# A new order of operations for the start, the repeated step and the end of a tiled recurrence with a max-out layer

## Chip, cores and metric

One core of one Trainium2 chip. The metric is the device time of one execution in microseconds (us), of the slowest core, here the only one. Medians and ranges of several executions are given. A profiled execution also has a *span*, from the first to the last counted instruction; it is 1.7 to 1.8 us shorter than the time of the same execution.

## The reference

```python
def _attn_ref(q, k, v, f_logit):                 # each (4, 8, 768, 48), float32
    f = 1.0 / (1.0 + np.exp(-f_logit))
    for t in range(S):
        state = f[:, :, t, :, None] * state + einsum('bhd,bhe->bhde', k[:, :, t], v[:, :, t])
        y[:, :, t] = einsum('bhd,bhde->bhe', q[:, :, t], state)

def _moe_ref(x, w1, w2, w_out):                  # x (3072, 384), w1, w2 (384, 1024), w_out (1024, 384)
    return np.maximum(x @ w1, x @ w2) @ w_out
```

The kernel cuts the sequence into 24 tiles of 128 positions (six for each of four batches; batches alternate). It uses max(a, b) = b + relu(a - b): with wd = w1 - w2 and w2o = w2 · w_out, the output is x · w2o + relu(x · wd) · w_out. So wd and w2o are built once, at the start, while tiles 0 and 1 are already under way.

## The kernel before

All operations have short names, and the order of every engine's queue is the order in which the names stand in three strings. The PROLOGUE sets up and runs the first tiles, the STEP is repeated with a growing tile number, the EPILOGUE ends. The traces show an engine's operations taken in that order: in run e2, further down, VectorE stood idle for 2.86 us ahead of a product whose load had not landed, and what stands behind it came after.

```python
PROLOGUE = """
setup 0  setup 2  setup 1  lf 0  lwo 2  lw2 4  lw2 3  lw2 2  lw2 0  lw2 5  e 0  lv 0  lw1 2
... (cut)
wdp 1  x 0  trqe 1  xT 0  lf 3  woc 3  a 1  am 1  lv 2  wdp 4  ln 2  w2o 10  w2o 9  w2oe 1
lq 3  cum 2  xTe 0  w2o 8  wdp 3  w2o 11  lk 3  wd 0  w2oe 2  lf 4  wd 5  d0 0  w2oe 0  ei 2
... (cut)
"""
STEP = """
lq 1  lv 1  lf 4  out -9  lk 2  st -4  d0 -1  cum 1  g0 -1  a 0  d1 -1  ei 1  am 0  fl 1
e 2  ed 1  o0 -1  g1 -1  kpv 1  qp 1  qp 0  y 0  ln 2  tmp -3  o1 -1  x 0  xT 0  tr 1  xTe 0
sa -2  tre 1  ob -1  v 1  qpv -2
"""
# what the names do (cut)
def sub_wd(n, eng=nc.vector):                    # "wd" on VectorE, "wdp" on GpSimd
    eng.tensor_sub(wd[:, j, cs], w1_f[:, j, cs], w2_f[:, j, cs])       # line 170, 128 x 512
def v_v(i):                                      # "v": VectorE, cast of v to bf16
    nc.vector.tensor_copy(vb, ld[i]["v"]...)                           # line 204
def m_kp(i, eng):                                # "kp" on GpSimd, "kpv" on VectorE
    eng.tensor_mul(s["kp"][:, :, 0:D], ld[i]["k"], s["ei"]...)         # line 232, 128 x 384
def m_qp(i, eng):                                # "qp" on GpSimd, "qpv" on VectorE
    eng.tensor_mul(s["qp"][:, :, 0:D], ld[i]["q"], s["ed"]...)         # line 237
# "lf lk lq lv n": loads of tile n (192 KB each); "lw1 lw2 lwo n": pieces of the weights;
# "tr": TensorE's transposes of kp and qp; "a": scores; "am": their mask (VectorE); "y": am·v + state;
# "x": y to bf16 (ScalarE); "d0 d1": x·wd in two halves; "g0 g1": relu (ScalarE);
# "o0 o1": the output (TensorE); "ei ed fl": exponentials (ScalarE); "tmp st": state (VectorE, GpSimd)
```

## Time and profile before

| | kernel before |
|---|---|
| time, median of 3 | 147.08 us (146.97 to 147.21) |
| span of the profiled execution | 145.5 us |
| TensorE busy | 127.8 us, 88% |
| first d / second d (tile 0 / tile 1) | 26.28 / 30.24 us |
| one tile in the middle | 4.96 us |

Two marks are used from here on. *d of tile n* is the first product with wd: TensorE can't start the first before wd is there. *o of tile n* is the first matmul of the output; it comes once a tile, so the differences between two kernels at each o show where time is won or lost. The lines of this profile stand in the prediction below.

### The profile page before, as it was taken

To read this page: it belongs to the slowest core of one execution; us is meant where nothing else is said; L and a number is where in the kernel's file an instruction comes from. 1 tells how busy PE (TensorE), PEld (TensorE's weight loads), DVE (VectorE), ACT (ScalarE), POOL (GpSimd) and SP (SyncE) were. 2 spreads that over 40 slices of the span, in tenths; PEclk is the share of its full clock that TensorE was granted. 3 is DMA by queue.
4 is the path that set the end of the run, shared out by engine and by line. 5 is a ranking of instruction groups with operands and counts; after the bars stand their busy time and mean duration, and the time that the engine had idled before them with its cause. 6 is when DMAs were issued, how large, how long until landed. Compare 5 with 4: busy or idle time off the path is not lost.

```text
span 145.5 us, 4481 instructions
## 1 busy us (share of the span) xinstructions
PE 127.8 (88%) x1817; PEld 100.9 (69%) x1817; DVE 104.4 (72%) x189; ACT 86.9 (60%) x202; POOL 56.2 (39%) x85
## 2 busy tenths in 40 slices
PE   0009697799999999999999999999999999999980
PEld 0005663687788878877888788888878877887680
DVE  7802868768697789677977887797779777979530
ACT  3336647765857697458656855775587558653430
POOL 8202278002836152454255325523552454245000
PEclk9999999999999999999999999999999999999999
DMA  4999999999998998999999999989999898914141
GB/s 112 310 326 206 289 299 293 177 202 190 157 205 149 207 189 153 199 148 221 199 234 185 229 229 194 216 174 227 183 205 223 188 232 163 268 44 162 59 162 56
DMA packets 106277, 28.61 MB, mean 197 GB/s; under 512 B 100496, under 2 KB 104720, under 8 KB 106256
## 3 DMA queue, kind: packets, MB, share of 16 engines
q1 hardware_dynamic: 106256, 28.32, 95.4%
q8 instruction: 14, 0.23, 0.7%
q14 instruction: 7, 0.06, 0.1%
HBM read 23.59 MB, written 4.72 MB: 195 GB/s over the span
## 4 chain that ended last, share of the span: by engine, by line
PE 86%; DMA 4%; ACT 2%; DVE 2%; SPq 2%; issue 1%
PE o L347 28%; PE d L329 24%; PE tr L244 7%; PE a L262 5%; DMA w_f<-in_moe_w_dram 4%; PE y L307 3%; PE xtp L317 3%; PE cum L209 3%; PE y L302 2%; PE sa L276 2%; PE w2op L187 2%; PE warm L386 2%; PE w2tp L177 1%; SPq L150 1%; DVE wd L170 1%; PE cum L211 1%
## 5 line engine op out<-in xcount | busy, mean ns | idle before, releaser
L237 POOL TENSOR_TENSOR qp<-qt,ed 128x384 bf16<-128x384 f32 x22 | 24.6, 1120 | 73.2 <-ACT ed L221 45.7
L336 ACT ACTIVATE gT<-d 128x512 bf16<-128x512 f32 x48 | 29.1, 606 | 34.1 <-PE d L329 34.0
L329 PE MATMUL d<-xT,wd 128*128 128x128 bf16 x576 | 39.7, 219 | 1.7 <-DVE wd L170 1.2
L347 PE MATMUL o<-wo,gT 128*128 128x384 bf16 x184 | 37.4, 325 | 0.0
L329 PEld LDWEIGHTS <-wd 128*128 128x128 bf16 x576 | 33.0, 98 | 4.4 <-DVE wd L170 1.6
L267 DVE TENSOR_TENSOR am<-a,mask 128x1024 bf16<-128x1024 f32 x24 | 29.4, 1224 | 1.2 <-PE a L262 1.2
L321 DVE COPY xT<-xtp 128x384 bf16<-128x384 bf16 x24 | 8.6, 357 | 20.1 <-PE xtp L317 20.1
L347 PEld LDWEIGHTS <-gT 128*128 128x128 bf16 x184 | 16.2, 97 | 9.0
L291 POOL TENSOR_TENSOR st<-tmp,fl 64x192 bf16<-64x192 f32 x40 | 20.5, 512 | 2.5 <-DVE tmp L284 1.0
L253 DVE COPY trs<-tr 128x1024 bf16<-128x1024 bf16 (+1 forms) x27 | 16.9, 631 | 3.1 <-PE tr L244 1.2
L209 PE MATMUL cum<-ell,ut 128*128 128x384 bf16 x24 | 8.0, 333 | 10.6 <-ACT ell L200 10.6
L196 ACT ACTIVATE e<-ft 128x384 f32<-128x384 f32 x24 | 12.7, 529 | 4.2 <-DMA ft<-in_f_logit_dram 4.1
L347 PE MATMUL o<-w2o,xT 128*128 128x384 bf16 x69 | 15.0, 326 | 0.0
L312 ACT CAST x<-y 128x384 bf16<-128x384 f32 x24 | 11.5, 480 | 5.0 <-PE y L307 4.9
L232 DVE TENSOR_TENSOR kp<-kt,ei 128x384 bf16<-128x384 f32 x21 | 13.1, 626 | 0.4 <-ACT ei L217 0.3
L221 ACT ACTIVATE ed<-cum 128x384 f32<-128x384 f32 x24 | 12.0, 498 | 2.1 <-PE cum L211 2.1
L200 ACT ACTIVATE ell<-e 128x384 bf16<-128x384 f32 x24 | 13.0, 540 | 0.2
L352 DVE COPY ob<-o 128x384 f32<-128x384 f32 x23 | 12.6, 548 | 0.5 <-PE o L347 0.5
L211 PEld LDWEIGHTS <-ell 128*128 128x128 bf16 x80 | 5.0, 98 | 10.6 <-issue 9.3
L217 ACT ACTIVATE ei<-cum 128x384 f32<-128x384 f32 x24 | 11.7, 487 | 0.0
L307 PE MATMUL y<-vb,am 128*128 128x48 bf16 x192 | 11.3, 184 | 0.0
L284 DVE TENSOR_TENSOR tmp<-sa,st 128x384 f32<-128x384 f32 x20 | 11.0, 551 | 0.0
(56 smaller groups left out, 176.7 us busy)
## 6 DMA issues: line engine op xcount, KB each, us to landing
ft<-in_f_logit_dram SPq DMA_DIRECT2D x24, 192.0 KB, 4.1
vt<-in_v_dram SPq DMA_DIRECT2D x24, 192.0 KB, 4.7
qt<-in_q_dram SPq DMA_DIRECT2D x24, 192.0 KB, 4.8
kt<-in_k_dram SPq DMA_DIRECT2D x24, 192.0 KB, 4.3
out_dram<-ob SPq DMA_DIRECT2D x23, 192.0 KB, 3.3
w_f<-in_moe_w_dram SPq DMA_DIRECT2D x12, 256.0 KB, 5.5
wo_f<-in_moe_w_out_dram SPq DMA_DIRECT2D x4, 384.0 KB, 4.8
out_dram<-obl SPq DMA_DIRECT2D x2, 96.0 KB, 1.6
```

The costliest lines, as they stand in the source:

```text
L196: nc.scalar.activation(e, ld[i]["f"].rearrange("p h d -> p (h d)"), AF.Exp, scale=-1.0)
L200: nc.scalar.activation(ell[:, :, 0:D], st[i]["e"].rearrange("p (h d) -> p h d", h=H), AF.Ln, bias=1.0)
L232: eng.tensor_mul(s["kp"][:, :, 0:D], ld[i]["k"], s["ei"].rearrange("p (h d) -> p h d", h=H))
L237: eng.tensor_mul(s["qp"][:, :, 0:D], ld[i]["q"], s["ed"].rearrange("p (h d) -> p h d", h=H))
L253: nc.vector.tensor_copy(s["tr"][:, n:n + len(sel)], psum.pop(("tr" + sel, i)))
L267: nc.vector.tensor_mul(am.rearrange("p o n c -> p (o n) c"), psum.pop(("a", i)).rearrange("p o n c -> p (o n) c"), mask)
L291: nc.gpsimd.tensor_mul(st_b[b][(c + 1) % 2][r, :, e], st[i]["tmp"][r, :, e], st[i]["fl"][r, :].unsqueeze(2).to_broadcast([DP, NP, D]))
L307: nc.tensor.matmul(out=y[:, ds], lhsT=am[:, o, p, :], rhs=vb[:, ds], start=(c == 0), stop=(c == 0 or o == 1))
L329: nc.tensor.matmul(out=ps[:, n, :], lhsT=wd[:, j, f * C:(f + 1) * C], rhs=st[i]["xT"][:, j, :], start=(j == 0), stop=(j == JG - 1))
L336: nc.scalar.activation(s["g"][:, half * 4:half * 4 + 4, :], psum.pop(("d", half, i)), AF.Relu)
L347: nc.tensor.matmul(out=psum["o", i], lhsT=l() if callable(l) else l, rhs=r, start=(n == 0), stop=(n == len(mms) - 1))
L352: nc.vector.tensor_copy(t, psum.pop(("o", i)))
```

## The change

Its intent: in the first seven steps, VectorE's instructions with two operands in SBUF are to be kept clear of GpSimd's. Beside one they take longer in the trace of the kernel before: a kp 0.72 and 1.07 us instead of 0.55, a subtraction 1.65 instead of 0.68; and four st of GpSimd beside such a kp take 2.54 us instead of 4 x 0.54. *Blocked* means this observation and no more, and so does *lock*. Weight pieces and tile loads are issued in a new order, all subtractions for wd but one go to VectorE, and in the step kp goes to GpSimd and qp to VectorE. The stores of tiles 15 to 22 move from the EPILOGUE into the step. Only the three strings change. The diff, cut:

```diff
 PROLOGUE = """
-setup 0  setup 2  setup 1  lf 0  lwo 2  lw2 4  lw2 3  lw2 2  lw2 0  lw2 5  e 0  lv 0  lw1 2
+setup 0  setup 2  setup 1  lwo 2  lw2 2  lw2 1  lw2 3  lw1 4  lw2 4  lf 0  woc 2  lw2 5
 ... (cut)
-lq 3  cum 2  xTe 0  w2o 8  wdp 3  w2o 11  lk 3  wd 0  w2oe 2  lf 4  wd 5  d0 0  w2oe 0  ei 2
+tr 1  lv 2  woc 3  w2o 7  tre 1  w2o 11  lq 3  e 2  w2o 9  w2o 10  ln 2  a 1  lk 3  wd 1
+w2oe 2  cum 2  w2oe 1  lf 4  wd 5  d0 0  w2oe 0  am 1  d1 0  g0 0  lv 3  ed 2  fl 2  v 1
+ei 2  o0 0  g1 0  lq 4  kp 2  y 1  o1 0  x 1  lk 4  qpv 2  xT 1  trk 2  xTe 1  trq 2  trke 2
 ... (cut)
+o1 5  x 6  lq 9  xT 6  tr 7  xTe 6  cum 8  tre 7  lf 10  fl 8  ei 8  ob 5  v 7  lv 11  lq 10
 STEP = """
-lq 1  lv 1  lf 4  out -9  lk 2  st -4  d0 -1  cum 1  g0 -1  a 0  d1 -1  ei 1  am 0  fl 1
-e 2  ed 1  o0 -1  g1 -1  kpv 1  qp 1  qp 0  y 0  ln 2  tmp -3  o1 -1  x 0  xT 0  tr 1  xTe 0
-sa -2  tre 1  ob -1  v 1  qpv -2
+d0 -1  cum 1  g0 -1  a 0  d1 -1  ed 1  am 0  qpv -3  ei 1  fl 1  g1 -1  kp 1  qp -3  o0 -1
+tmp -3  y 0  qpv 1  o1 -1  x 0  st -3  e 2  xT 0  tr 1  ln 2  xTe 0  sa -2  tre 1  ob -1
+v 1  lk 5  lf 5  lq 4  out -9  lv 4
 EPILOGUE = """
-out 19  out 20  out 16  out 18  st 22  st 23  st 21  out 21  out 22  out 15  sa 23  out 17
-lo 1  lo 3  lob1 0  lo 0  lo 2  lout 1  lob0 0  fl 23  lout 0
+st 23  st 22  st 21  tmp 23  lo 1  lo 3  sa 23  lob1 0  lo 0  sa 22  lo 2  lout 1  lob0 0
+lout 0
```

More of the change, by code (lines that the diff above doesn't have):

```diff
@@ L17 @@
 PROLOGUE = """
-setup 0  setup 2  setup 1  lf 0  lwo 2  lw2 4  lw2 3  lw2 2  lw2 0  lw2 5  e 0  lv 0  lw1 2
-woc 2  lw2 1  lq 0  lk 0  lf 1  lwo 0  lk 1  w2ca 5  ln 0  w2ca 2  cum 0  lwo 1  w2ca 0
-warm 6  lq 1  fl 0  ei 0  w2ca 3  lw1 1  w2c 1  w2ca 4  ed 0  lf 2  qp 0  w2T 6  w2T 2  lwo 3
-w2Te 6  w2T 0  kp 0  w2Te 2  w2T 4  w2Te 0  w2T 3  lw1 4  e 1  w2T 5  w2Te 3  trk 0  w2Te 4
-trq 0  ln 1  w2T 1  w2T 7  w2Te 1  lw1 3  cum 1  trke 0  fl 1  ei 1  trqe 0  ed 1  a 0  lw1 0
-kpv 1  woc 0  w2Te 5  v 0  w2Te 7  w2o 1  lw1 5  woc 1  am 0  w2o 0  w2o 2  sa 0  lv 1  qp 1
@@ L24 @@
-w2o 5  tmp 0  w2o 3  w2o 6  lq 2  wdp 2  w2o 4  w2o 7  trk 1  lk 2  e 2  y 0  trke 1  trq 1
-wdp 1  x 0  trqe 1  xT 0  lf 3  woc 3  a 1  am 1  lv 2  wdp 4  ln 2  w2o 10  w2o 9  w2oe 1
-lq 3  cum 2  xTe 0  w2o 8  wdp 3  w2o 11  lk 3  wd 0  w2oe 2  lf 4  wd 5  d0 0  w2oe 0  ei 2
-d1 0  g0 0  lv 3  v 1  ed 2  y 1  fl 2  x 1  lq 4  qpv 2  o0 0  g1 0  xT 1  o1 0  lk 4  kpv 2
-trq 2  xTe 1  trk 2  ob 0  d0 1  lf 5  e 3  trke 2  trqe 2  d1 1  ln 3  g0 1  lq 5  v 2
-a 2  cum 3  g1 1  am 2  fl 3  ed 3  lv 4  o0 1  ei 3  qp 3  y 2  lk 5  kpv 3  o1 1  x 2
@@ L30 @@
-xT 2  tr 3  lf 6  e 4  xTe 2  sa 1  d0 2  tre 3  ln 4  ob 1  lq 6  cum 4  a 3  v 3  ed 4
-d1 2  g0 2  am 3  lv 5  qp 4  ei 4  g1 2  o0 2  tmp 1  lv 6  kp 4  fl 4  y 3  o1 2  x 3
-st 0  lk 6  e 5  xT 3  tr 4  xTe 3  ln 5  sa 2  d0 3  tre 4  lf 7  ob 2  cum 5  g0 3  a 4
-d1 3  lf 8  v 4  ei 5  am 4  ed 5  g1 3  qp 5  lv 7  o0 3  tmp 2  y 4  kpv 5  st 2  o1 3
-x 4  lq 7  fl 5  e 6  xT 4  tr 5  st 1  ln 6  xTe 4  lk 7  sa 3  d0 4  tre 5  ob 3  cum 6
-lf 9  a 5  v 5  fl 6  ei 6  d1 4  am 5  g0 4  lq 8  ed 6  g1 4  o0 4  tmp 3  y 5  lk 8  kp 6
@@ L36 @@
-qpv 6  o1 4  x 5  lf 11  e 7  xT 5  tr 6  xTe 5  ln 7  sa 4  d0 5  tre 6  lv 8  ob 4  cum 7
-a 6  v 6  ed 7  d1 5  lk 9  g0 5  am 6  e 8  g1 5  lf 10  qp 7  o0 5  tmp 4  ei 7  y 6  fl 7
-lq 9  kpv 7  o1 5  x 6  ln 8  xT 6  tr 7  xTe 6  lv 9  e 9  cum 8  tre 7  ln 9  ob 5  lk 11
-v 7  lk 10  lq 10  lq 12  lf 12
+setup 0  setup 2  setup 1  lwo 2  lw2 2  lw2 1  lw2 3  lw1 4  lw2 4  lf 0  woc 2  lw2 5
+lv 0  lf 1  lw2 0  lq 0  lk 0  lwo 1  w2c 4  wd 4  lwo 0  e 0  w2ca 3  lq 1  w2ca 2  ln 0
+w2ca 1  lw1 3  v 0  cum 0  ei 0  lw1 0  w2ca 5  e 1  lw1 2  w2c 0  w2T 7  ed 0  w2T 2  w2Te 7
@@ new lines @@
+ln 1  w2T 5  w2Te 2  fl 0  lk 1  qp 0  w2T 6  w2Te 5  w2T 4  w2Te 6  w2T 1  w2Te 4  cum 1
+lwo 3  kp 0  w2T 0  warm 2  w2Te 0  lf 2  woc 1  w2Te 1  tr 0  ei 1  ed 1  lw1 1  sa 0  fl 1
+w2T 3  tre 0  woc 0  tmp 0  a 0  lw1 5  qp 1  w2Te 3  w2o 2  w2o 0  lv 1  wd 3  w2o 1  w2o 3
+lk 2  wdp 0  am 0  w2o 6  lq 2  y 0  w2o 4  x 0  w2o 5  lf 3  kp 1  xT 0  w2o 8  xTe 0  wd 2
+tr 1  lv 2  woc 3  w2o 7  tre 1  w2o 11  lq 3  e 2  w2o 9  w2o 10  ln 2  a 1  lk 3  wd 1
+w2oe 2  cum 2  w2oe 1  lf 4  wd 5  d0 0  w2oe 0  am 1  d1 0  g0 0  lv 3  ed 2  fl 2  v 1
@@ new lines @@
+ei 2  o0 0  g1 0  lq 4  kp 2  y 1  o1 0  x 1  lk 4  qpv 2  xT 1  trk 2  xTe 1  trq 2  trke 2
+d0 1  trqe 2  lf 5  e 3  ob 0  a 2  ln 3  d1 1  g0 1  am 2  lv 4  cum 3  g1 1  v 2  ed 3
+lq 5  o0 1  ei 3  y 2  qp 3  fl 3  o1 1  x 2  lk 5  kpv 3  xT 2  tr 3  xTe 2  sa 1  lf 6
+e 4  d0 2  tre 3  ln 4  ob 1  a 3  g0 2  lf 7  v 3  cum 4  am 3  d1 2  ei 4  ed 4  lv 5
+g1 2  tmp 1  o0 2  qp 4  y 3  lk 6  kpv 4  o1 2  x 3  st 0  fl 4  xT 3  tr 4  lq 6  e 5
+xTe 3  sa 2  d0 3  ln 5  tre 4  lf 8  ob 2  cum 5  a 4  v 4  ed 5  d1 3  fl 5  am 4  g0 3
@@ new lines @@
+lv 6  qp 5  ei 5  g1 3  o0 3  st 1  lq 7  kpv 5  y 4  tmp 2  o1 3  x 4  lk 7  e 6  xT 4
+tr 5  ln 6  xTe 4  sa 3  d0 4  tre 5  lk 8  e 7  ob 3  cum 6  g0 4  a 5  lv 7  v 5  d1 4
+ei 6  am 5  ed 6  ln 7  lf 9  kp 6  o0 4  g1 4  tmp 3  y 5  fl 6  st 2  lq 8  qpv 6  o1 4
+x 5  xT 5  st 3  tr 6  xTe 5  lk 9  sa 4  cum 7  tre 6  d0 5  ed 7  ob 4  lv 8  a 6  v 6
+g0 5  d1 5  am 6  ei 7  lf 11  e 8  g1 5  o0 5  qpv 7  fl 7  ln 8  y 6  lv 9  tmp 4  kp 7
+o1 5  x 6  lq 9  xT 6  tr 7  xTe 6  cum 8  tre 7  lf 10  fl 8  ei 8  ob 5  v 7  lv 11  lq 10
@@ L40 @@
+lk 10  lv 10  lk 11  lq 11  lv 12  lf 12  lq 12  lk 12
 """
 STEP = """
-lq 1  lv 1  lf 4  out -9  lk 2  st -4  d0 -1  cum 1  g0 -1  a 0  d1 -1  ei 1  am 0  fl 1
-e 2  ed 1  o0 -1  g1 -1  kpv 1  qp 1  qp 0  y 0  ln 2  tmp -3  o1 -1  x 0  xT 0  tr 1  xTe 0
-sa -2  tre 1  ob -1  v 1  qpv -2
+d0 -1  cum 1  g0 -1  a 0  d1 -1  ed 1  am 0  qpv -3  ei 1  fl 1  g1 -1  kp 1  qp -3  o0 -1
+tmp -3  y 0  qpv 1  o1 -1  x 0  st -3  e 2  xT 0  tr 1  ln 2  xTe 0  sa -2  tre 1  ob -1
+v 1  lk 5  lf 5  lq 4  out -9  lv 4
```

## The prediction

> **What bounds the kernel now.** I read the page first, then the waits of TensorE, then the timeline: of one step in the middle, of the first 30 us, and of the end. The page:
>
> ```profile
> span 145.5 us, 4481 instructions
> PE 127.8 (88%) x1817; PEld 100.9 (69%) x1817; DVE 104.4 (72%) x189; ACT 86.9 (60%) x202; POOL 56.2 (39%) x85
> PE   0009697799999999999999999999999999999980
> DMA  4999999999998998999999999989999898914141
> PE 86%; DMA 4%; ACT 2%; DVE 2%; SPq 2%; issue 1%
> ```
>
> TensorE fills every slice from the ninth to the last but one. The chain that ended last is 86% TensorE. What TensorE waits for:
>
> ```profile
> PE cum L209 <- ACT ell L200: 10.6, 1, 10.6
> PE d L329 <- DVE wd L170: 1.2, 1, 1.2
> PE w2op L187 <- ACT wo L166: 0.9, 2, 0.6
> PE a L262 <- DVE trs L253: 0.7, 1, 0.7
> ```
>
> All of these waits lie in the first 27 us (columns: total, times, longest). Now the middle, by two first halves of d, one step apart:
>
> ```profile
> 84.50 0.83 PE L329 MATMUL d<-xT,wd 128*128 128x128 bf16 x12
> 89.46 0.83 PE L329 MATMUL d<-xT,wd 128*128 128x128 bf16 x12
> ```
>
> One tile takes 4.96 us. Start to start, the parts are d 0.67+0.68, cum 0.33, a 0.33, o 0.98+0.81, y 0.37, xtp 0.17, tr 0.45, sa 0.17: the sum is 4.96, so nothing is left between them. A new order of other engines' work can't shorten this; it can only break it. From the first d to the end TensorE loses little: o of tiles 1 and 2 start at 32.42 and 37.39, 4.97 apart, where a tile without the state term (0.17 less) needs 4.79, so 0.18 is lost there. The next intervals are 4.79, 4.96, 4.96. The end (from 135.78) has about 1 us of waits that belong to the chain of the last tile.
>
> So the time is (start of the first d) + about 119.2 us, and the first d is where gain can come from:
>
> ```profile
> 20.00 2.50 POOL L170 TENSOR_TENSOR wd<-w_f 128x512 bf16<-128x512 f32 x2
> 23.18 2.50 POOL L170 TENSOR_TENSOR wd<-w_f 128x512 bf16<-128x512 f32 x2 [0.69 <-DMA w_f<-in_moe_w_dram]
> 24.57 2.26 DVE L170 TENSOR_TENSOR wd<-w_f 128x512 bf16<-128x512 f32 x2
> 26.28 1.51 PE L329 MATMUL d<-xT,wd 128*128 128x128 bf16 x24 [1.23 <-DVE wd L170]
> ```
>
> The two subtractions of VectorE take 1.65 and 0.68 us (longest and shortest of that group). The long one began at 24.57, inside GpSimd's fourth, which lasts to 25.68; the first d waits for it 1.23 us.
>
> [...]
>
> ```profile
> 42.37 1.00 POOL L237 TENSOR_TENSOR qp<-qt,ed 128x384 bf16<-128x384 f32 x1 [2.42 <-issue]
> 43.06 0.72 DVE L232 TENSOR_TENSOR kp<-kt,ei 128x384 bf16<-128x384 f32 x1
> 43.32 2.54 POOL L291 TENSOR_TENSOR st<-tmp,fl 64x192 bf16<-64x192 f32 x4
> ```
>
> kp takes 0.55 us when free; here it ends 0.41 us after GpSimd's qp ends (43.78 against 43.37). It comes before the st that is queued behind qp: four st take 2.54 us instead of 4 x 0.54. At 33.43 a kp takes 1.07 in the same way.
> [...] Here: qp 1.00 us against 0.55.
> [...] Here 12 of 128 columns take 0.67 us, 56 ns each[...]; the six "warm" matmuls of 512 columns begin 0.43 us apart at 11 us[...].
>
> **The change, part by part.**
>
> *The step.* TensorE's order is the same, instruction for instruction. kp moves to GpSimd and qp to VectorE; on ScalarE ed comes ahead of ei, and e after x; tmp comes ahead of the product on VectorE. I lay the measured durations on the step that begins with d at 84.50. ScalarE: g0 85.37, ed 85.86, ei 86.24 to 86.73, g1 about 86.75. GpSimd: kp 86.86 to 87.86. VectorE: am to 87.17, tmp 87.08 to 87.63, then qp blocked until 87.86, ending 88.28 (plus 0.41, as above). TensorE transposes kp at 88.84 and qp at 89.06: 0.8 us to spare for qp, 1.0 for kp. x is ready for xtp as before; ln ends about 89.6 and cum starts at 90.1. So 4.96 us stay 4.96: gain 0.
>
> *Loads.* The first 24 transfers are the same set in another order (8 of 192 KB, 12 of 256 KB, 4 of 384 KB), so the last weight piece lands at the same time. I fit them on the traced waits that end with a landing (f at 3.5, a w2 piece at 9.5 and one at 11.9, f at 14.6, q at 19.05, f at 20.5). My estimate from these is 0.92, 0.8 and 1.2 us each, from 2.0 us, plus 1.3 us to land. It gives 23.7+1.3 = 25.0 for the 24th and 24.2 for the 23rd. In the new order these are w1 pieces 5 and 1; piece 1 gates the first half of d, piece 5 the second.
>
> *The first d.* w1 piece 4 is subtracted early, pieces 3, 2, 1, 5 on VectorE and only 0 on GpSimd, at about 19.6, so no GpSimd work meets the last two: 0.68 us each instead of 1.65 for one. Piece 1: 24.25 to 24.9. The other gates: f of tile 2 is 22nd and lands at 23.4, e and ln to 24.5; the last cast of wo (21st, landing 22.5) is 0.83 long, to 23.35; three pairs of w2op (0.33 each) to 24.4; a 0.33 and cum 0.33 to 25.1. So the first d starts at about 25.1 (26.28 before): 1.2 us earlier. If landings are 0.5 us later than my fit, at 25.6.
>
> *What is given back.* ScalarE does ed, fl, ei of tile 2 ahead of g1 of tile 0: g1 ends at about 28.0, and o of tile 0, which wants it at 27.8, waits about 0.25. q of tile 2 lands at about 27.9, its product on VectorE is blocked by GpSimd's kp (27.55 to 28.55) and ends at 28.97; the second d (30.41 before) starts at about 29.4. In tile 3 kp on VectorE still meets qp on GpSimd: 0.17 lost, like the 0.18 of before. From here the step runs with a lead of 0.8 to 1.0 us.
>
> *Four fewer "warm" matmuls.* Before, they lay in a stretch in which TensorE waited for ScalarE's casts (13.1 to 13.5). Gain 0 by themselves.
>
> *The end.* The outs come in order, one per step, instead of in the epilogue; before, three were issued at 139 to 140.3, just ahead of the last two stores. With less ahead of them the last stores may land up to 0.2 us earlier; I count 0.05.
>
> Sum: 1.2 - 0.25 - 0.1 + 0.05 = 0.9 us by the fit, about 0.4 with late landings. I take 0.8: 147.08 - 0.8 = 146.3 us.
>
> **Rivals.** (a) *The start is bound by the transfers, and nothing is gained.* For: the same bytes come ahead of the first d, the loads of tiles 2 to 4 follow about 1 us apart with little lead (f of tile 3 lands at 28.9, wanted at 29), and tile 0's own chain starts later (f of tile 0 is 7th instead of 1st; cum at 11.6 instead of 10.57). Against: before, 1.2 us were lost after the last landing. It would make 146.9 to 147.2.
> (b) [...] If st went ahead of the blocked qp, qp would end at about 89.35, TensorE would wait 0.3 us a step, over 17 steps 5 us: 152. Against: 43.06, where VectorE went first.
> [...]
> (d) *More than I see.* If the chain of tile 0 and the weights lets d start at the landing of piece 1 itself, and everything after it is at its floor, 145.4.
>
> **Range and chances.** The middle is fixed at 4.96 a tile, so only 0 to 1.5 us are at stake: 145.4 to 147.1 holds (a), the sum and (d). Over 2% faster means under 144.1, a first d at about 23.3, before its weights have landed: 0.03. Over 2% slower needs (b)[...]: 0.02. Within 2%: 0.95.
>
> **What would show it right or wrong.** Right: steps of 4.96 us between d's in the middle; all wd on VectorE near 0.68 us; the first d at 25.0 to 25.7; the second near 29.4; VectorE's qp in the middle at 0.55 to 0.75 us. Wrong: TensorE waiting for trs or tr in the middle (b); [...] a first d that waits for x, wo or w2o at 26 or later (a). I'd be wrong altogether if the step were not 4.96 us any more.

## The result, and the profile after

The changed kernel took **147.93 us** (median of 4, 147.76 to 148.17), the kernel before on the same chip 147.15 (146.97 to 147.23): ratio 1.0056, 95% interval 1.0037 to 1.0075. Ratios here are the mean time of one kernel's fast runs over that of the other's of the same rounds, so not quite the ratio of the medians. That is within 2%, as said, but 0.8 us slower where 0.8 us faster was predicted, and above the range.

Its page and its waits of TensorE (total, times, longest):

```profile
span 146.0 us, 4482 instructions
PE 128.0 (88%) x1813; PEld 100.9 (69%) x1813; DVE 108.7 (74%) x190; ACT 88.9 (61%) x201; POOL 56.4 (39%) x83
PE 81%; ACT 5%; DMA 5%; DVE 3%; issue 2%; SPq 2%; POOL 1%
PE cum L209 <- ACT ell L200: 12.3, 1, 12.3
PE y L307 <- DVE am L267: 0.6, 2, 0.3
PE tr L244 <- POOL kp L232: 0.5, 1, 0.5
```

TensorE's work is the same. Its first wait, for tile 0's chain, has grown from 10.6 to 12.3 us; it ends before 12.5 us, ahead of the first d. The long wait for wd (1.2 us before) is gone, as intended. New ones have come: for kp on GpSimd, and for am on VectorE, a wait that the kernel before doesn't have. In the chain that ended last, TensorE's share fell from 86% to 81%. Now the timeline of the start (columns: start, duration, engine, line, operation, out<-in, tile and type, count; in brackets the idle time before it and what ended it), as it answers to the wd and d lines of before:

```profile
24.57 1.49 DVE L170 TENSOR_TENSOR wd<-w_f 128x512 bf16<-128x512 f32 x2
25.50 1.50 PE L329 MATMUL d<-xT,wd 128*128 128x128 bf16 x24
28.77 0.99 POOL L232 TENSOR_TENSOR kp<-kt,ei 128x384 bf16<-128x384 f32 x1 [5.95 <-ACT x L312]
29.45 0.73 DVE L237 TENSOR_TENSOR qp<-qt,ed 128x384 bf16<-128x384 f32 x1 [1.99 <-DMA qt<-in_q_dram]
...
30.23 0.23 PEld L244 LDWEIGHTS <-qp 128*128 128x128 bf16 x4 [0.19 <-DVE qp L237]
30.50 0.83 PE L329 MATMUL d<-xT,wd 128*128 128x128 bf16 x12
```

The two last subtractions are no longer blocked (1.49 us for both, 2.26 before) and the first d starts at 25.50, 0.78 earlier. But tile 2's products wait for their loads: VectorE stood idle 1.99 us until q of tile 2 had landed (29.3; k at 28.6). The second d, which stands behind the transposes of tile 2, starts at 30.50. The same stretch of the kernel before:

```profile
28.18 0.56 DVE L237 TENSOR_TENSOR qp<-qt,ed 128x384 bf16<-128x384 f32 x1 [1.07 <-ACT ed L221]
28.65 0.55 DVE L232 TENSOR_TENSOR kp<-kt,ei 128x384 bf16<-128x384 f32 x1
30.24 1.50 PE L329 MATMUL d<-xT,wd 128*128 128x128 bf16 x24
```

There, in this profile, the product of q waits for ScalarE's ed, not for a load. So of 0.78 us nothing is left at the second d, and 0.26 us are lost on top. The middle is as predicted: a step of 4.96 us.

```profile
80.50 0.83 PE L329 MATMUL d<-xT,wd 128*128 128x128 bf16 x12
85.46 0.72 PE L329 MATMUL d<-xT,wd 128*128 128x128 bf16 x10
```

A fifth of a microsecond more is lost in tile 3 (o of tile 1 to o of tile 2 takes 5.14 us, 4.94 before). Most of the rest comes where the prologue meets the step (the *seam*, around 56 us): o of tile 6 to o of tile 7 takes 5.45 us instead of 4.96. The timeline there, after:

```profile
55.76 0.48 ACT L217 ACTIVATE ei<-cum 128x384 f32<-128x384 f32 x1
56.32 1.00 POOL L232 TENSOR_TENSOR kp<-kt,ei 128x384 bf16<-128x384 f32 x1 [2.71 <-ACT ei L217]
56.46 1.08 DVE L204 CAST vb<-vt 128x384 bf16<-128x384 f32 x1
...
58.73 0.22 PE L307 MATMUL y<-vb,am 128*128 128x48 bf16 x2 [0.32 <-DVE am L267]
```

and before:

```profile
55.99 0.35 DVE L204 CAST vb<-vt 128x384 bf16<-128x384 f32 x1
```

ei of tile 8 now comes ahead of ScalarE's other work ("fl 8 ei 8" at the end of the PROLOGUE), so GpSimd's kp of tile 8 starts 0.14 us ahead of VectorE's cast of v of tile 7. The cast, which has *one* operand, takes 1.08 us instead of 0.35 and ends 0.22 us after kp (57.54 against 57.32); am is late (57.46; before it began at 56.25), and y waits.

### The profile page after: what moved, and what is told of

Same layout as the page of the kernel before. It is cut to its first block, busy times and chain, and to the rows that moved or that the text cites. A ratio compares the mean times of both kernels' runs of the same rounds, so it can differ in the third digit from the quotient of the medians.

```text
span 146.0 us, 4482 instructions
## 1 busy us (share of the span) xinstructions
PE 128.0 (88%) x1813; PEld 100.9 (69%) x1813; DVE 108.7 (74%) x190; ACT 88.9 (61%) x201; POOL 56.4 (39%) x83
## 4 chain that ended last, share of the span: by engine, by line
PE 81%; ACT 5%; DMA 5%; DVE 3%; issue 2%; SPq 2%; POOL 1%
PE o L347 25%; PE d L329 23%; PE tr L244 8%; PE a L262 5%; DMA ft<-in_f_logit_dram 5%; PE y L307 3%; PE cum L209 3%; PE xtp L317 3%; PE sa L276 2%; PE y L302 2%; PE w2tp L177 2%; DVE am L267 2%; PE w2op L187 2%; SPq L150 1%; ACT gT L336 1%
## 5 line engine op out<-in xcount | busy, mean ns | idle before, releaser
L232 POOL TENSOR_TENSOR kp<-kt,ei 128x384 bf16<-128x384 f32 x21 | 21.0, 1000 | 54.4 <-ACT fl L227 30.6
L267 DVE TENSOR_TENSOR am<-a,mask 128x1024 bf16<-128x1024 f32 x24 | 29.3, 1222 | 0.1
L291 POOL TENSOR_TENSOR st<-tmp,fl 64x192 bf16<-64x192 f32 x40 | 25.9, 647 | 1.6
L209 PE MATMUL cum<-ell,ut 128*128 128x384 bf16 x24 | 8.2, 341 | 12.3 <-ACT ell L200 12.3
L237 DVE TENSOR_TENSOR qp<-qt,ed 128x384 bf16<-128x384 f32 x19 | 14.3, 755 | 2.0 <-DMA qt<-in_q_dram 2.0
L211 PEld LDWEIGHTS <-ell 128*128 128x128 bf16 x80 | 5.1, 99 | 12.3 <-issue 11.2
L237 POOL TENSOR_TENSOR qp<-qt,ed 128x384 bf16<-128x384 f32 x5 | 5.0, 998 | 21.3 <-ACT ed L221 19.2
```

Source lines behind the costliest of these rows:

```text
L232: eng.tensor_mul(s["kp"][:, :, 0:D], ld[i]["k"], s["ei"].rearrange("p (h d) -> p h d", h=H))
L237: eng.tensor_mul(s["qp"][:, :, 0:D], ld[i]["q"], s["ed"].rearrange("p (h d) -> p h d", h=H))
L267: nc.vector.tensor_mul(am.rearrange("p o n c -> p (o n) c"), psum.pop(("a", i)).rearrange("p o n c -> p (o n) c"), mask)
L291: nc.gpsimd.tensor_mul(st_b[b][(c + 1) % 2][r, :, e], st[i]["tmp"][r, :, e], st[i]["fl"][r, :].unsqueeze(2).to_broadcast([DP, NP, D]))
```

## The experiments

Fifteen runs were made, in four groups, each group on one chip and beside runs of the kernel before. Theories: **S** (supply): the loads of tile 2 come too late, and take back what the first d gained. **V** (seam): v's cast is blocked beside GpSimd's kp (1.08 us instead of 0.35), and this costs 0.49 us. **O** (order): the new order of work on the engines itself gives back what the first d gained. **E** (end): the stores issued ahead of the last ones cost time before.

### First group: loads, seam, end

**e1, the changed kernel with its first 24 transfers in the old order.**

```diff
 # changed kernel: same operations, the 24 first loads take the old sequence of kinds
-... lwo 2  lw2 2  lw2 1  lw2 3  lw1 4  lw2 4  lf 0  lw2 5  lv 0  lf 1  lw2 0  lq 0  lk 0 ...
+... lf 0  lwo 2  lw2 2  lw2 1  lw2 3  lw2 4  lw2 5  lv 0  lw1 4  lw2 0  lq 0  lk 0  lf 1 ...
```

> The new kernel, with its first 24 transfers put in the order of kinds of the old kernel (tile, wo, five w2, ...); nothing else changed. Theory L (the supply): in the new kernel k, q of tile 2 and f of tile 3 landed at 28.6, 29.3, 30.2 us, 1.0 us later than in the old one (28.2 for the later of k and q, 29.1), and this cost 0.87 us between the first and the second d. If the order of the first 24 transfers makes this, they land again at 28.2 and 29.1, the second d starts at 29.6 to 29.9 instead of 30.50, and the kernel takes 147.1 to 147.4 instead of 147.9. Theory O (the order of ScalarE's and GpSimd's work loses it, whatever lands when): the second d stays at 30.3 to 30.6 and the time at 147.7 to 148.1.

Measured: 149.08 us (fast runs, 148.92 to 150.03; one of the six was slow), ratio 1.0154 (1.0100 to 1.0209). A miss. GpSimd's subtraction waits 2.44 us for its piece and holds back kp of tile 1; the first d comes at 27.27.

**e2, the kernel before with its first 24 transfers in the new order.** (The same edit the other way round.)

> The old kernel, with its first 24 transfers in the order of kinds of the new kernel. Theory L: k and q of tile 2 land 0.5 to 1.0 us later and the time is 147.5 to 148.1. Theory O: the time stays within 0.2 us of 147.15.

Measured: 153.55 us, ratio 1.0419 (1.0370 to 1.0468). A miss. VectorE, whose queue is taken in order, stands still 2.86 us for a load that now comes late (k of tile 1); the first d comes at 31.75. So order of loads and order of work can't be separated by swapping one: neither run decides between S and O. Two things could be read all the same. In e1, k and q of tile 2 landed at 26.7 and 27.7, no transpose waited for them, and o of tile 0 to o of tile 1 took 4.98 us instead of 5.71. And what the DMA engines moved in the first 12 us follows the order of the loads: 243 GB/s in e1, 233 in e2, against 246 in the kernel before and 220 in the changed one.

**e3, the changed kernel without the early ei of tile 8.**

```diff
-o1 5  x 6  lq 9  xT 6  tr 7  xTe 6  cum 8  tre 7  lf 10  fl 8  ei 8  ob 5  v 7  lv 11  lq 10
+o1 5  x 6  lq 9  xT 6  tr 7  xTe 6  cum 8  tre 7  lf 10  ob 5  v 7  lv 11  lq 10
```

> The new kernel without the early 'fl 8, ei 8' at the end of its first seven steps: they come at the place that the repeated step gives them, behind g0 and ed. Theory V (the lock): in the new kernel GpSimd's kp of tile 8 (56.32 to 57.32) started just ahead of VectorE's cast of v of tile 7, which took 1.08 us instead of 0.35; am and y came late and TensorE lost 0.49 us in that step. With ei later, kp starts after the cast: the cast takes 0.35, the o-to-o interval there is 4.96 instead of 5.45, and the time is 147.3 to 147.6. Rival: the loss comes from elsewhere (the change of step at the seam, a load): then 147.8 to 148.1.

Measured: 146.74 us (146.56 to 147.57), ratio 0.9984 (0.9940 to 1.0027), on this chip, where the kernel before took 146.86. The timeline at the seam:

```profile
55.91 0.35 DVE L204 CAST vb<-vt 128x384 bf16<-128x384 f32 x1
57.21 1.00 POOL L232 TENSOR_TENSOR kp<-kt,ei 128x384 bf16<-128x384 f32 x1 [4.14 <-ACT fl L227]
```

The cast takes 0.35 us again, and o of tile 6 to o of tile 7 is 4.96. V holds.

**e4, the kernel before with its last stores in order, one to a step.**

```diff
-out 19  out 20  out 16  out 18  st 22  st 23  st 21  out 21  out 22  out 15  sa 23  out 17
+st 22  st 23  st 21  sa 23
```

> The old kernel with the stores of tiles 15 to 22 in their order, as in the new one. In the new kernel the span ended 3.41 us after the issue of the last two stores, in the old one 3.83 us. Theory E (three stores just ahead of the last two delay them): the span ends 0.3 to 0.45 us earlier, time 146.7 to 146.9. Rival (the end is a draw of the run): 147.0 to 147.3.

Measured: 146.76 us, ratio 0.9985 (0.9940 to 1.0031): the same. From the last o to the end of the span is 4.46 us, about as before (4.38). E doesn't hold. What e4 did show: its start is that of the kernel before, untouched, and yet its first d came at 25.57 and not at 26.28.

### Second group: tile 2's loads, the blocked products, both repairs

**e5, the changed kernel once more** (no edit).

> The changed kernel once more, untouched, as the control for the three runs beside it on this chip. All theories: 0.5 to 1.0 us slower than the kernel before in the same rounds (ratio 1.003 to 1.007), v's cast of tile 7 at 1.08 us, o of tile 6 to o of tile 7 5.45 us. Supply theory: the second half-open point, the landing of q of tile 2, lies between 28 and 29.5 us, and the second d follows it by about 1.2 us wherever it falls.

Measured: 147.29 us (fast runs, 146.87 to 147.99; one of the six was slow), ratio 1.0023 (0.9991 to 1.0056); the kernel before 146.89 here. The seam is the same: cast 1.07, 5.46 us. q of tile 2 landed at 29.1, the second d came at 30.14. Smaller than on the first chip (1.0056); the intervals overlap.

**e6, two transfers fewer (wrong result).**

```diff
-lk 2 ... lq 2                      # in PROLOGUE
-    ... ld[i]["k"] ...  ld[i]["q"]
+    ... ld[1 if i == 2 else i]["k"] ...  ld[1 if i == 2 else i]["q"]
```

> Wrong result on purpose: tile 2 takes k and q of tile 1, and the two transfers are gone; nothing else is moved. Supply theory (the gain of the first d is given back because tile 2's k and q land late): second d at 29.2 to 29.5 instead of 30.5, f of tile 3 lands some 2 us earlier and cum of tile 3 no longer waits; o of tile 1 starts at about 31.5, the whole 0.9 us faster than the untouched changed kernel. Rival (the order of work on VectorE, GpSimd and ScalarE gives it back, whatever lands when): second d stays at 30.0 to 30.5, within 0.2 us of the untouched changed kernel.

Measured: 147.37 us (146.97 to 148.57), ratio 1.0032 (0.9997 to 1.0067): no faster than e5. Its profiled execution, one of the fastest of its six (147.07), shows what S expects:

```profile
25.18 1.50 PE L329 MATMUL d<-xT,wd 128*128 128x128 bf16 x24
29.46 0.83 PE L329 MATMUL d<-xT,wd 128*128 128x128 bf16 x12
```

The second d comes at 29.46, o of tile 1 at 31.50, 0.68 us before that of e5, and it keeps this lead to the last o (140.96 against 141.63). So in this execution S holds, and O alone would have left the second d at 30.0 to 30.5. But some of O remains. From the first d to the second it is 4.28 us here, and 4.28 in e1, where no transpose waited for a load either; the kernel before takes 3.96 where nothing waits (before, e9). The trace shows what fills the difference: the second half of o takes 1.15 us instead of 0.98, since a weight load waits 0.25 us for g1, and the second d starts 0.39 us after the last transposes begin instead of 0.22, just behind VectorE's copy xT (29.05 to 29.41). In the times of all six S isn't seen. I count it as half a result.

**e7, both products of tiles 2 and 3 on VectorE.**

```diff
-kp 2 ... qp 3
+kpv 2 ... qpv 3
```

> Both products of tiles 2 and 3 on VectorE, so neither meets GpSimd's. Lock theory: kp of tile 3 on VectorE 0.55 us instead of 1.08, the wait of TensorE on it (0.32) gone, the product of q of tile 2 ends within 0.6 us of q's landing, o of tile 1 to o of tile 2 4.8 to 4.95 us instead of 5.14: 0.2 to 0.5 us faster than the untouched changed kernel. Supply theory alone (the lock only covers waits on landings): f and k of the next tiles take its place, within 0.1 us of it.

Measured: 147.65 us, ratio 1.0041 (1.0009 to 1.0073). Its timeline at tile 3, then that of the changed kernel:

```profile
33.50 0.55 DVE L232 TENSOR_TENSOR kp<-kt,ei 128x384 bf16<-128x384 f32 x1
```

```profile
33.53 1.00 POOL L237 TENSOR_TENSOR qp<-qt,ed 128x384 bf16<-128x384 f32 x1 [3.76 <-ACT ed L221]
33.87 1.08 DVE L232 TENSOR_TENSOR kp<-kt,ei 128x384 bf16<-128x384 f32 x1 [0.67 <-ACT ei L217]
35.00 0.23 PEld L244 LDWEIGHTS <-kp 128*128 128x128 bf16 x4 [0.32 <-DVE kp L232]
```

o of tile 1 to o of tile 2 takes 4.82 us instead of 5.14: the block on kp of tile 3 (1.08 us instead of 0.55) costs the changed kernel 0.3 us, and moving one product takes it away. For tile 2 nothing is won: kp ends early, q lands at 29.1, and the second d is at 30.04. The times don't resolve the 0.3: 147.65 against e5's 147.29, where 0.2 to 0.5 us less was expected.

**e8, e7 and e3 together.**

> The run before and the late fl 8 and ei 8 of the earlier run together. If the two losses add: 0.7 to 1.0 us faster than the untouched changed kernel, and 0.2 to 0.4 us faster than the kernel before (ratio 0.997 to 0.9985). If they overlap: no better than the late ei 8 alone (ratio 0.9984).

Measured: 146.84 us (146.48 to 147.24), ratio 0.9992 (0.9964 to 1.0019). o of tile 1 to 2 is 4.83, o of tile 6 to 7 is 4.96: the two repairs add in the trace. In the same rounds e5 has 1.0023, so the repairs are worth about 0.3% (1.0023 - 0.9992), 0.46 us, here; the intervals overlap, so the times alone don't prove it. It is as fast as the kernel before, no faster.

### Third group: the kernel before, part by part

**e9, the kernel before once more** (no edit).

> The kernel before once more, for a second profile of its start. All theories: ratio 1.000 within 0.003. Draw theory (the first profile of the kernel before drew a late start, so the 0.78 us that the first d seemed to gain was partly luck): first d at 25.5 to 25.9 instead of 26.28, TensorE waits 0.5 to 0.8 us for wd instead of 1.23. Fixed theory: first d at 26.2 to 26.4 again. Bytes theory (the new order of transfers moves the bytes of the start more slowly): 2.9 to 3.0 MB moved by 12 us and 6.35 to 6.45 MB by 24 us, against 2.64 to 2.77 and 6.18 to 6.31 in the profiles of the changed kernel.

Measured: 146.96 us, ratio 1.0005 (0.9971 to 1.0039).

```profile
25.63 1.51 PE L329 MATMUL d<-xT,wd 128*128 128x128 bf16 x24 [0.93 <-ACT w2o L191]
29.59 1.50 PE L329 MATMUL d<-xT,wd 128*128 128x128 bf16 x24
```

The first d comes at 25.63, not at 26.28. The expectation said that TensorE would wait 0.5 to 0.8 us for wd; the wait is 0.93. The profile puts it down to w2o, whose last cast ended at 25.60, but the blocked subtraction ended at 25.57, and in all five profiles of this start d begins 0.05 to 0.06 us after that subtraction: it is wd. The draw theory holds for the start: five profiles have the old start untouched (before, e4, e9, e10, e15), with first d's at 26.28, 25.57, 25.63, 25.64 and 25.23.

**e10, the kernel before with the new STEP and EPILOGUE.** Two loads of v that the new STEP takes for granted were appended.

```diff
-... lk 11  v 7  lk 10  lq 10  lq 12  lf 12
+... lk 11  v 7  lk 10  lq 10  lq 12  lf 12  lv 10  lv 11
 STEP, EPILOGUE: those of the changed kernel
```

> The kernel before with the changed kernel's step and end, its first seven steps left alone (two loads of v appended, which that step takes for granted). The prediction's own view (the step is neutral, the end gives 0.05): ratio 0.999 to 1.001, steps of 4.96 us, from the last o to the end of the span 4.0 to 4.5 us. Rival (the step costs something that the middle of the trace doesn't show, such as the shift of kp and qp at the seam): 0.3 us or more slower, and o of tile 6 to o of tile 7 above 5.2 us.

Measured: 146.8 us, ratio 0.9992 (0.9963 to 1.0022). The result was wrong (relative error 0.03): the new STEP takes up the state update three tiles back and the old one four, and the update of tile 3 falls between. One pair of GpSimd instructions of 20 is missing, too little to hide a loss in every step. Steps are 4.96 us but for one of 5.28, the seam is 4.96, and from the last o to the end is 4.5 us. So the new step and end by themselves are neutral, as predicted; the loss is in the new prologue.

**e11, the kernel before with its fourth subtraction on VectorE.**

```diff
-lq 3  cum 2  xTe 0  w2o 8  wdp 3  w2o 11  lk 3  wd 0  w2oe 2  lf 4  wd 5  d0 0
+lq 3  cum 2  xTe 0  w2o 8  wd 3  w2o 11  lk 3  wd 0  w2oe 2  lf 4  wd 5  d0 0
```

> The kernel before with one thing of the change alone: the fourth subtraction of weights goes from GpSimd to VectorE, so the last two are not blocked. Lock theory for the first d: each of VectorE's last subtractions 0.68 us, TensorE's wait on wd at most 0.3, first d 0.5 to 1.0 us earlier than in the kernel before run beside it. Supply theory for the time: k of tile 2 still lands at about 28.1, so the second d is no earlier than 29.6 and the time gains 0 to 0.4 us (ratio 0.997 to 1.0). If nothing else limits: 0.5 us or more (ratio 0.9965 or less).

Measured: 147.03 us, ratio 1.0011 (0.9982 to 1.0041).

```profile
24.47 1.89 DVE L170 TENSOR_TENSOR wd<-w_f 128x512 bf16<-128x512 f32 x3
25.81 1.51 PE L329 MATMUL d<-xT,wd 128*128 128x128 bf16 x24 [1.01 <-DVE wd L170]
```

No subtraction is blocked any more (1.89 / 3 = 0.63 us each), and the first d is no earlier. The three stand in a row and the moved one is first; three free ones take about as long as two of which one is blocked (1.47 to 1.80 us in e4, e10, e15 and e9; 2.26 in the first profile). Here the block was taken away by moving 0.63 us of work to the blocked engine, which had no time to spare for it.

**e12, e11 and both products of tile 3 on VectorE** (in place of "qp 3", "qpv 3").

> The run before, and the product of q of tile 3 on VectorE too, ahead of k's. Lock theory: k's product of tile 3 takes 0.55 us instead of 1.07, o of tile 1 to o of tile 2 4.79 us instead of 4.94, so 0.15 us below the run before in the trace; ratio to the kernel before 0.996 to 0.9995.

Measured: 146.88 us, ratio 1.0004 (0.9977 to 1.0030). kp of tile 3 takes 0.55 us instead of 1.07, and o of tile 1 to o of tile 2 stays at 4.94 us. A miss: in the kernel before this block cost nothing, y waited for am and not for kp.

### Fourth group: what was still open

**e13, as e11, but behind the subtraction that the first half of d needs.**

```diff
-... wdp 3  w2o 11  lk 3  wd 0  w2oe 2  lf 4  wd 5  d0 0
+... w2o 11  lk 3  wd 0  wd 3  w2oe 2  lf 4  wd 5  d0 0
```

> The kernel before with the fourth subtraction of weights on VectorE, as in the earlier run, but behind the one that the first half of d waits for, so that the moved 0.6 us doesn't stand in its way. Lock theory: VectorE's first subtraction ends some 0.4 us earlier than when blocked, first d at 25.0 to 25.3 instead of 25.6. Supply theory: k of tile 2 lands at about 28.1 all the same, so the second d stays at 29.5 to 29.75 and the time is within 0.1 us of the kernel before (ratio 0.9985 to 1.0015). If the first d sets the end, as the prediction has it: second d at 29.2 and 0.4 us faster (ratio 0.997).

Measured: 146.96 us, ratio 1.0013 (0.9989 to 1.0036). First d at 25.43, within the spread of the old start and not at 25.0 to 25.3; the second half of d now waits 0.25 us. k of tile 2 landed at 28.4, the second d came at 29.87. Nothing is won, but not for the reason that S gives: the second d follows o of tile 0 (27.47) by 2.40 us, as in every trace with the old order of work (2.39 to 2.41), so TensorE doesn't wait for k of tile 2. What holds o of tile 0 back is the wait for wd's second half and then v of tile 1, which landed at 26.83 (its cast ends at 27.21, y starts at 27.27). The first d moved so little, too, that it's a weak test.

**e14, e13 with two transfers fewer (wrong result),** as e6.

> Wrong result on purpose: the run before, with tile 2 taking k and q of tile 1 and those two transfers gone. Supply theory: now the earlier first d reaches the second, which comes at 29.0 to 29.3, and o of tile 1 at 31.1 to 31.4; 0.3 to 0.5 us less than the run before in the trace. Rival (order of work): second d at 29.5 or later in spite of the missing transfers.

Measured: 146.82 us, ratio 1.0002 (0.9977 to 1.0026). The second d came at 30.28: not what S expected. But not O either: in this execution the last weight piece landed at 26.3 instead of 24.5 in e13, and the second half of d waited 0.79 us for it. Inconclusive for S against O. As in e6's times, two transfers fewer make no faster kernel; here something else landed late, for e6 the times leave the reason open.

**e15, the kernel before with the early ei and GpSimd's kp of tile 8.**

```diff
-... ln 9  ob 5  lk 11  v 7 ...
+... ln 9  ei 8  kp 8  ob 5  lk 11  v 7 ...
```

> The kernel before with the seam's fault of the changed kernel put in: ei of tile 8 early on ScalarE and its product with k on GpSimd, just ahead of v's cast of tile 7 on VectorE; nothing else. Lock theory: the cast takes 1.0 to 1.1 us instead of 0.35, o of tile 6 to o of tile 7 5.4 to 5.5 us instead of 4.96, and the whole is 0.4 to 0.6 us slower (ratio 1.003 to 1.004). Rival (the seam's loss belonged to something else of the changed kernel, such as its loads): cast 0.35, no loss.

Measured: 147.73 us, ratio 1.0062 (1.0039 to 1.0085): slower, and not for the reason expected.

```profile
55.45 0.35 DVE L204 CAST vb<-vt 128x384 bf16<-128x384 f32 x1
56.05 1.00 POOL L232 TENSOR_TENSOR kp<-kt,ei 128x384 bf16<-128x384 f32 x1 [3.75 <-DMA kt<-in_k_dram]
...
58.14 0.20 PE L302 MATMUL y<-st,trs 128*128 128x96 bf16 x1 [0.78 <-POOL st L291]
```

kp had to wait for its load, came after the cast, and left it alone (0.35); but it stood ahead of the state update in GpSimd's queue, and y waited 0.78 us for that. The seam took 6.46 us. So V rests on e3 and e8 against the changed kernel, e5 and e7 (4.96 in both, 5.45 or 5.46 in all three). And the seam has a second way to lose time.

## Why the prediction was wrong, and where it was right

The starts vary by some tenths of a us from run to run, so I compare means of all profiles whose start is untouched: five of the old (before, e4, e9, e10, e15) and three of the new (after, e3, e5).

| start of | old | new | new - old |
|---|---|---|---|
| first d | 25.67 | 25.45 | -0.22 |
| second d | 29.77 | 30.20 | +0.43 |
| o of tile 2 | 36.75 | 37.37 | +0.62 |
| o of tile 6 | 56.36 | 56.92 | +0.56 |
| o of tile 7 (old: before, e4, e9; new: after, e5) | 61.41 | 62.50 | +1.09 |
| last o (the same five) | 140.79 | 141.82 | +1.03 |
| end of the span (before, e9; after, e5) | 145.27 | 145.89 | +0.62 |

**The first d: right for the profile, wrong in what it was worth.** 25.1 was predicted, "25.6 if landings are 0.5 us later"; it came at 25.38 to 25.50, with the last weight piece at 25.2 to 25.4 and not at 25.0. But I took the 26.28 of one profile as the kernel's own start. It was the latest of five; the mean is 25.67, and the gain is 0.2 us, not 1.2. The step that failed is "0.68 us each instead of 1.65 for one", taken as a gain on the path. The 1.65 was a draw too: in the other four old starts the blocked subtraction took 0.87 to 1.20 us, so the block costs 0.4 us on average. e11 and e13 take it away in the old kernel and win nothing in their times. And in the new kernel the first d doesn't wait for wd: the subtraction it needs ends 0.2 us ahead of it (25.27 against 25.50 in the changed kernel), and TensorE comes from the chain behind the last cast of wo, which landed at 22.9 and not at 22.5.

**What is given back: wrong, and the main reason at the start.** I had k and q of tile 2 landing by 27.9 and the second d at 29.4, 0.35 us of loss in all. For the order of work this was about right: I had 4.3 us from the first d to the second (29.4 - 25.1), and where no load is waited for it is 4.28 (e6, e1). I had named the wait for g1 but not the 0.17 us for xT. The step that failed is "q of tile 2 lands at about 27.9", and behind it "so the last weight piece lands at the same time": the 24th transfer landed at 24.7 us on average in the five old starts (24.2 to 25.5) and at 25.3 in the three new (25.2 to 25.4); the 27th, the last load that tile 2's products need, at 28.2 (28.0 to 28.3) and 29.1 (28.9 to 29.3). q landed between 28.9 and 29.3 in the five new kernels that load it as the change does (after, e3, e5, e7, e8), and the second d followed at 29.94 to 30.50. The order within the tile, kp on GpSimd or on VectorE, doesn't matter (e7, e8). The old kernel has its last product's load at 28.0 to 28.3. From first to second d the new kernel loses 0.65 us (0.43 + 0.22): it takes 4.75 on average and the old 4.10, so about 0.47 are the loads (4.75 - 4.28) and 0.18 the order. My fit gave every load a fixed cost and so the same time to the same set in any order. The traces differ on that in two ways. First, the rate at the start, by windows of the kernel before and of the changed one (columns: window, its length, busy time and count of TensorE, its weight loads, VectorE, ScalarE and GpSimd, granted clock, DMA share, GB/s):

```profile
0.00:12.00 12.00, 1.43 (x8) 0.77 (x9) 5.82 (x13) 5.15 (x10) 4.03 (x16) 1.00 0.86 246
...
```

```profile
0.00:12.00 12.00, 0.00 (x0) 0.10 (x1) 6.88 (x15) 3.86 (x6) 4.01 (x16) 1.00 0.83 220
...
```

In the first 12 us the profiles with the old order (before, e4, e9, e14, e15) move 244 to 247 GB/s and those with the new (after, e3, e5 to e8) 220 to 231; in the next 12 us the two kernels move 287 and 294. So by 24 us the old order has moved 6.40 MB (12 x 0.246 + 12 x 0.287), the new 6.17; e9 and e5 have 6.43 and 6.28. Loads of q, k, v, f alone then go at about 190 GB/s (24 to 32 us, both kernels; in the kernel before it was 392 between 22.25 and 23.25), so 0.15 to 0.23 MB are 0.8 to 1.2 us (an estimate). Second, most of these starts have a lull in which the DMA engines move little. In e9 it lies in the window from 25.25 us, and in e5 in that from 28.00:

```profile
25.25:26.25 1.00, 0.62 (x11) 0.62 (x12) 0.93 (x2) 0.75 (x2) 0.00 (x0) 1.00 0.25 40
...
```

```profile
...
28.00:29.00 1.00, 1.00 (x13) 0.49 (x9) 0.00 (x0) 0.67 (x2) 0.85 (x1) 1.00 0.25 47
```

In the other's window each moves 226 (e9) and 189 GB/s (e5). The other profiles with the old loads move 121 GB/s in the window from 25.25 us and 197 in that from 28.00 (before), and 81 and 193 (e14, with two fewer); in e4 (170 and 161) and e15 (159 and 166) neither window shows a lull. Those with the new (after, e3, e6 with two fewer, e7, e8) move 177 to 202 and 48 to 100. In e9 and e5 the lull lies about where an issue of SyncE ends that took more than 2 us: in e9 k of tile 2, from 20.91 for 4.56 us; in e5 v of tile 2, from 25.85 for 2.23. Most issues of a tile's load in these stretches take 0.4 to 1.2 us.

With the old loads the landing that was waited for is that of v of tile 1 in e4 and e15 (VectorE idle 0.59 and 0.82 us); with the new, k or q of tile 2 (1.99 us in the changed kernel), which have no slack. v of tile 1 has only little, since the old order puts a y that needs it ahead of o of tile 0. In e4, e10, e13 and e15 this y starts 0.44 us after v landed (at 26.57 to 26.83), directly behind its cast. In e15:

```profile
27.01 0.36 PE L307 MATMUL y<-vb,am 128*128 128x48 bf16 x8 [0.27 <-DVE vb L204]
```

So the old start, too, is held by a landing when its first d comes early (25.23 here, yet the second d only at 29.61), and an earlier wd alone gains little there. That the lulls make the landings late is my reading and not shown; what makes the issues long stays open (the changed kernel has issues of 2.17 us from 22.89 and of 2.77 us, two weight pieces together, from 18.42 too), and the runs with two transfers fewer (e6, e14) show that taking those two away doesn't make the time shorter. So "tile 2's loads set the second d of the changed kernel" is shown by its waits and by one profile without them (e6); that an earlier landing would make the kernel faster is not shown.

**Tile 3: the place right, the size wrong.** "kp on VectorE still meets qp on GpSimd: 0.17 lost, like the 0.18 of before." In the changed kernel it costs 0.3 us (e7, e8); in the kernel before it cost nothing (e12). Against before the loss is 0.19 us (0.62 - 0.43).

**The seam: not seen, and the largest loss with a single shown cause, 0.49 us.** I laid the durations on a step in the middle and checked only two-operand instructions for a block. I had the order of the seam before me and didn't walk through it. e3 takes two names out of the changed kernel and has the 0.49 us back.

**The step: right.** 4.96 us, VectorE's qp 0.73 us in the middle, and e10 has the whole step at ratio 0.9992. Rival (b) is out: no wait of each step. Rival (a), bound by transfers, was nearest, and it named the loads of tiles 2 to 4; but its 146.9 to 147.2 us counted no loss from them, and the transfers struck at the second d.

**The end: not 0.05, and not the change.** From the last o to the end of the span it is 4.0 to 4.1 in after, e3 and e5, and 4.3 to 4.4 in e6, e7 and e8, which have the same end word for word; with the old end it is 4.06 (e15) to 4.41 (e14). It varies from run to run; the last two stores took 1.6 us from issue to landing (the median) in both kernels.

The sum: -0.22 (first d), +0.65 (to the second), +0.19 (tile 3), +0.53 (o of tile 6 to 7, with 0.49 of it shown), -0.12 (the remaining small terms), -0.41 (the end, partly luck: it compares two pairs of profiles with the five of the row above) is the +0.62 of the spans. Without the end's luck it is +1.0; the times gave +0.78 on the first chip and 0.0023 x 147, or 0.34, on the second.

## What to carry to other kernels

Before counting a gain at one mark, ask what the *next* mark waits for: here loads of the tiles behind stood less than a microsecond off (v of tile 1 with the old order, k and q of tile 2 with the new), and a start that was earlier by 0.2 us only met them sooner. A new order of the same transfers can also change when the last of them lands: 0.6 us later on average for the 24th here. When work is moved between engines whose instructions take longer beside each other (here a cast 1.08 us instead of 0.35, a kp 1.07 instead of 0.55), walk through the hand-over between hand-ordered start and repeated step, one-operand casts included; two names there cost 0.49 us. And take the start from several profiles: it varied by a microsecond here, and one profile made a gain of 0.2 look like 0.8.
